# Decode attention plus MLP on one core: the last rows of w2 loaded in three even transfers instead of seven partly uneven ones, and the MLP's first bias in five transfers instead of one

## The chip, the core and the metric

The kernel runs on one core of a Trainium2 chip. The metric is the device time of one execution in microseconds (us), as the median over several executions. "The profile" is one execution recorded by the hardware profiler; its times count from the start of that execution's span.

## What is computed

The kernel is one decode step for two sequences (B = 2, one new token each, width D = 576): the input, plus attention over a sliding window of a key/value cache, plus an MLP with squared ReLU. Both branches read the same layer-normed input. All tensors are bf16.

```python
W = min(4096, max(256, Sk // 4))            # 2048 of the 8192 cached positions
xn = _layernorm(x)
q = xn @ wq                                 # [2, 576] @ [576, 4096], 32 heads of 128
k, v = last W positions of the caches       # 16 heads, each for two heads of q
o = softmax(q k^T * 128 ** -0.5) @ v
attn = o @ wo                               # [2, 4096] @ [4096, 576]
h = relu(xn @ w1 + b1) ** 2                 # [2, 576] @ [576, 4608]
mlp = h @ w2 + b2                           # [2, 4608] @ [4608, 576]
out = x + attn + mlp
```

There are only two rows of activations, so nearly all of the work is reading: 53.6 MB of caches and weights from HBM, each byte once.

## The kernel before

**Units.** The attention is cut into eight units (four groups of four key/value heads, times two sequences). Unit u has one 2 MB tile of K and one of V, `k_u` and `v_u`, each loaded by one transfer of 128 partitions x 16 KB. `step(u)` transposes K on TensorE in eight groups (`transposes`, copied out of PSUM by ScalarE in L276 and VectorE in L278), forms the scores and the softmax, and carries along the product with V of unit u - 2. K and V tiles share a pool of six buffers, so the load of a later tile waits until TensorE has read the tile whose buffer it takes.

**Weights.** `issue_flat` loads wq, w1 and wo (4.5 to 5.2 MB each) as one flat transfer each. w1 and wo use the buffer that wq had, so wo is issued when the first MLP product (`mlp_h`, which adds the bias b1 by a matmul) has read w1.

**w2.** Its 4608 rows are seen as two halves of 128 partitions x 18 rows (`w2_rows`); one row of one partition is 576 elements, 1152 B, and a partition's 18 rows of a half lie next to each other in HBM. The first half is one tile, `w2a` (20736 B per partition). The second half is split: rows 0 to 8 go to `w2b` (10368 B per partition, in a buffer of the K/V pool), rows 9 to 17 to `w2c`, a buffer of its own. `W2P` (L76) lists the pieces of `w2c` as ranges of rows, and `issue_w2c` (L215) issues them. The piece of rows 12 to 15 is issued as four transfers over the partition ranges of `XS`: 0 to 24, 25 to 29, 30 to 125, 126 to 127. All other pieces cover 128 partitions.

**Queues.** The large transfers are issued by SyncE, in the order k0, wq, k1, v0, k2, v1, k3, v2, ..., w1, k7, v6, v7, wo, w2a, w2b, then the pieces of w2c, and run in the profile's queue q1. ScalarE issues four small ones (queue q10): x, the bias b1 (L423; 8 rows of 1152 B), the bias b2 (L424) and the output. Every transfer signals one of eight DMA semaphores, which the tile framework hands out in turn over both queues, in the order in which it places the transfers. A transfer whose semaphore is still in use by the transfer eight places before waits on its issuing engine until that one has landed.

**The end.** `out_acc` multiplies a row of activations, one per partition, with one row of weights per partition and adds into `out_ps`: four matmuls of 144 columns. The order is: the 32 rows of wo, the 18 rows of w2a, then rows 0 to 17 of the second half, of which 0 to 8 read `w2b` and 9 to 17 read `w2c`. ScalarE copies `out_ps` (L459) and issues the output's transfer (L460).

```python
for r in range(FR):
    w, o = (w2b_sb, r) if r < R9 else (w2c_sb, r - R9)
    out_acc(hT_sb[:, 1, r, :], w, o, stop=(r == FR - 1))
```

Of the kernel before, what the change touches and what calls it, by code (L numbers as in the profile page):

```python
# [16 lines left out]
def kernel(  # L17
# [14 lines left out]
    nc = tc.nc  # L32
    P = 128
    B, Sq, D = A_x.shape
# [38 lines left out]
    WC = Dh // WR  # L73
    FR = L1 // P
    assert HW == 32 * FR and QH * 2 == NC and NC * WC == 32
    W2P = [(9, 12), (12, 16), (16, 17), (17, 18)]  # L76
    R9 = 9
    XR = (12, 16)
    XS = [(0, 25), (25, 30), (30, 126), (126, 128)]
    BS = 16  # L80
    MB = BS * (B - 1) + 1
    RM = 32 * (NG4 - 1) + MB
# [99 lines left out]
    for t0, half, k0, n, pc in ((0, 0, 0, NK, 0), (0, 1, 0, NK, 1), (1, 0, 1, NK - 1, 1), (1, 1, 0, NK - 1, 0)):  # L182
# [11 lines left out]
                          in_=own[:].unsqueeze(2).to_broadcast([P, NC, WC]))  # L194
# [11 lines left out]
                          in_=ident[0:2 * NG4, 0:2 * NG4].rearrange("p (x g) -> p x g", g=NG4).unsqueeze(3)  # L206
                          .to_broadcast([2 * NG4, 2, NG4, B]))

    b1_sb = const.tile([2 * NG4, HW], BF16, name="b1_sb")
    w2_rows = B_w2.rearrange("(x p r) n -> x p (r n)", x=2, r=FR)  # L210


    w2c_sb = w2pool.tile([P, (FR - R9) * D], BF16, name="w2c")

    def issue_w2c(r0, r1, q):  # L215
        for p0, p1 in XS if (r0, r1) == XR else [(0, P)]:
            q.dma_start(out=w2c_sb[p0:p1, (r0 - R9) * D:(r1 - R9) * D], in_=w2_rows[1, p0:p1, r0 * D:r1 * D])

    out_ps = psum.tile([RM, OQ], F32, tag="out", name="out_ps")
    nc.vector.memset(out_ps[:], 0.0)  # L220
# [172 lines left out]
    def step(u):  # L393
        fin = None
        w = u - 2
        with_pv = w >= 0
        for g in range(NG):
            transposes(u, g)
            if with_pv and g == 1:
                pv(w, 0, 2)  # L400
            if with_pv and g == 2:
                pv(w, 1, 2)
                fin = pv_end(w)
            if g == TG + 1:
                scores(u, 0)
            if g == TG + 2 and fin:
                fin()
        scores(u, 1)
        softmax(u)
# [10 lines left out]
    softmax(0)  # L420
    load_v(2)
    b1_rows = B_b1.rearrange("(x n) -> x n", n=HW)
    nc.scalar.dma_start(out=b1_sb[:], in_=b1_rows)  # L423
    nc.scalar.dma_start(out=xb_sb[B:B + 1, :], in_=B_b2.rearrange("(o n) -> o n", o=1))  # L424
    step(1)
    load_k(4)
# [16 lines left out]
    nc.sync.dma_start(out=w2a_sb[:], in_=w2_rows[0])  # L443
    nc.sync.dma_start(out=w2b_sb[:], in_=w2_rows[1, :, 0:R9 * D])
    for r0, r1 in W2P:
        issue_w2c(r0, r1, nc.sync)
    step(NU - 1)
    pv_all(NU - 2)
    pv_all(NU - 1)
# [41 lines left out]
```

## Time and profile before

| | |
|---|---|
| three executions | 135.7, 136.2, 136.22 us; median 136.2 |
| the profiled execution | 135.7 us, of which the span is 133.8 |
| read from HBM | 53.62 MB, 401 GB/s over the span |
| TensorE busy | 86.7 us, 65% of the span |
| VectorE, ScalarE busy | 63.0 and 46.5 us, 47% and 35% |
| DMA queue q1 (SyncE's transfers) | 95.1% of 16 engines' span |
| DMA queue q8 (instructions) | 7 packets, 0.3% |

The span's slices in the page are 1/40 of it each, 3.35 us. The row "DMA" gives the mean busy share of the core's 16 DMA engines in tenths, the row "GB/s" what they moved in that slice. The chain of work that ended last is followed back from the last instruction; its shares tell what the end was waiting for. A table of stages gives for each stretch the busy time of PE, PEld, DVE, ACT and POOL with the count of instructions, then the granted TensorE clock, the DMA share (1 is all 16 engines) and GB/s. In a list of instructions in order of time, the columns are start, duration, engine, line, operation and operands, and in brackets the idle time before it with what ended it. In a list of waits, the numbers after the colon are the total in us, how often, and the longest. Beside these views, the trace has a record of each DMA packet (start, duration, bytes, queue) and of each landing on a DMA semaphore.

### The profile page before, as it was taken

How to read it: one execution, taken by the hardware profiler on the slowest of the kernel's cores; microseconds unless marked ns; L12 is line 12 of the kernel's file. 1: busy time of each engine (PE TensorE's matmuls, PEld its weight loads, DVE VectorE, ACT ScalarE, POOL GpSimd, SP SyncE). 2: the span in 40 equal slices, each digit the busy share in tenths (PEclk: the TensorE clock that was granted, in tenths of full speed). 3: DMA queues.
4: the chain of work that ended last, by engine and by line, in shares of the span. 5: the costliest groups of instructions: out<-in, count | busy, mean ns of one | idle time of the engine just before them, and what ended most of it. 6: DMA issues, size and time to landing. Idle time of an engine off the chain costs nothing.

```text
span 133.8 us, 2285 instructions
## 1 busy us (share of the span) xinstructions
PE 86.7 (65%) x949; PEld 52.4 (39%) x949; DVE 63.0 (47%) x176; ACT 46.5 (35%) x67; POOL 4.9 (4%) x15
## 2 busy tenths in 40 slices
PE   0079429699589777796797986007659962469351
PEld 0069302266346353443363452004255621159230
DVE  7754400326457667496547496300364776620000
ACT  6715400328656185283535373200206522000000
POOL 5000000010010100100100100100000001000000
PEclk9999955558999999999779999755686998555955
DMA  4999899999999999999999999989999989899960
GB/s 148 397 439 518 364 406 431 431 431 421 433 431 426 441 416 436 426 436 426 436 421 431 466 505 409 402 385 416 446 416 476 457 375 507 382 409 396 307 168 1
DMA packets 3655, 53.76 MB, mean 402 GB/s; under 512 B 435, under 2 KB 702, under 8 KB 958
## 3 DMA queue, kind: packets, MB, share of 16 engines
q1 hardware_dynamic: 3612, 53.61, 95.1%
q8 instruction: 7, 0.11, 0.3%
q10 hardware_dynamic: 34, 0.02, 0.0%
q14 instruction: 2, 0.02, 0.0%
HBM read 53.62 MB, written 0.00 MB: 401 GB/s over the span
## 4 chain that ended last, share of the span: by engine, by line
DMA 74%; PE 15%; ACT 5%; DVE 2%; issue 1%; SPq 0%; POOL 0%; ACTq 0%; DVEq 0%
DMA v<-in_A_v_cache_dram 24%; DMA w2c<-in_B_w_dram 22%; DMA k<-in_A_k_cache_dram 15%; DMA wq<-in_A_wq_dram 13%; PE kT_ps L99 6%; PE q_ps L96 3%; ACT kT L276 3%; PE sc_ps L96 3%; PE o_ps L96 1%; ACT p L308 1%; ACT L308 1%; PE qT_ps L99 1%; PE out_ps L96 1%; DVE m L297 1%; DVE qrow L244 1%
## 5 line engine op out<-in xcount | busy, mean ns | idle before, releaser
L99 PE MATMUL kT_ps<-ident_f,k 128*128 128x128 f32 x256 | 41.2, 311 | 5.3 <-DMA k<-in_A_k_cache_dram 2.7
L99 PEld LDWEIGHTS kT_ps<-ident_f,k 128*128 128x128 f32 x256 | 32.6, 159 | 19.2 <-issue 8.8
L276 ACT COPY kT<-kT_ps 128x1024 bf16<-128x1024 bf16 x32 | 31.8, 1012 | 18.9 <-PE kT_ps L99 18.9
L278 DVE COPY kT<-kT_ps 128x1024 bf16<-128x1024 bf16 x32 | 21.8, 680 | 6.5 <-PE kT_ps L99 6.2
L96 PE MATMUL sc_ps<-kT,qz 128*32 128x512 bf16 x128 | 10.5, 413 | 6.5 <-DVE kT L278 4.7
L308 ACT ACTIVATE p<-sc_ps,bias 128x512 bf16<-128x512 f32 x8 | 5.5, 687 | 21.3 <-DVE gown L304 21.3
L96 PE MATMUL o_ps<-v,pT 128*32 128x512 bf16 x128 | 11.9, 454 | 0.0
L96 PEld LDWEIGHTS <-xnT 128*4 128x4 bf16 x108 | 3.6, 121 | 16.4 <-issue 14.8
L96 PE MATMUL h_ps<-w,xnT 128*4 128x288 bf16 x72 | 4.5, 443 | 8.0 <-DMA w<-in_B_w_dram 8.0
L311 DVE STREAM_TRANSPOSE pT<-p 128x512 bf16<-128x512 bf16 x8 | 5.7, 711 | 6.2 <-ACT p L308 6.2
L341 DVE SCALAR_TENSOR_TENSOR o<-o_ps,in_s,o 128x128 f32<-128x128 f32 x24 | 8.3, 345 | 0.4
L297 DVE TENSOR_REDUCE m<-sc_ps 128x1 f32<-128x512 f32 x8 | 5.5, 691 | 5.5 <-PE sc_ps L96 5.5
L381 DVE TENSOR_TENSOR hrow<-t 100x1152 bf16<-100x1152 f32 x2 | 2.6, 1354 | 9.7 <-ACT t L379 9.7
L459 ACT CAST fin_sb<-out_ps 113x144 bf16<-113x144 f32 x1 | 0.3, 278 | 19.1 <-PE out_ps L96 19.1
L96 PE MATMUL q_ps<-wq,xnT 128*4 128x512 bf16 x36 | 4.0, 627 | 4.4 <-DMA wq<-in_A_wq_dram 4.4
L301 POOL PARTITION_ALL_REDUCE gmax<-m x8 | 2.9, 365 | 105.4 <-DVE m L299 105.4
L96 PE MATMUL op_ps<-o,of_h 128*32 128x129 f32 x16 | 3.7, 316 | 4.6 <-DVE o L341 4.6
L96 PEld LDWEIGHTS <-qz 128*32 128x32 bf16 x128 | 2.2, 98 | 10.7 <-DVE kT L278 7.2
L99 PE MATMUL pro_ps<-ident,xn_sb 2*128 2x2 bf16 x5 | 0.9, 180 | 6.8 <-DVE xn_sb L173 6.5
L96 PEld LDWEIGHTS <-hT_sb 128*17 128x17 bf16 x144 | 3.3, 109 | 4.8 <-issue 4.8
L96 PE MATMUL out_ps<-wo,ws 128*17 128x144 bf16 x128 | 4.0, 324 | 1.2 <-DVE ws L357 1.2
L339 DVE TENSOR_SCALAR o<-o_ps,in_s 128x128 f32<-128x128 f32 x8 | 2.7, 341 | 3.7 <-PE o_ps L96 3.7
(71 smaller groups left out, 56.0 us busy)
## 6 DMA issues: line engine op xcount, KB each, us to landing
k<-in_A_k_cache_dram SPq DMA_DIRECT2D x8, 2048.0 KB, 21.2
v<-in_A_v_cache_dram SPq DMA_DIRECT2D x8, 2048.0 KB, 23.7
w<-in_B_w_dram SPq DMA_DIRECT2D x1, 5184.0 KB
wq<-in_A_wq_dram SPq DMA_DIRECT2D x1, 4608.0 KB
wo<-in_A_wo_dram SPq DMA_DIRECT2D x1, 4608.0 KB, 20.9
w2a<-in_B_w_dram SPq DMA_DIRECT2D x1, 2592.0 KB, 26.7
w2b<-in_B_w_dram SPq DMA_DIRECT2D x1, 1296.0 KB
w2c<-in_B_w_dram SPq DMA_DIRECT2D x2, 432.0 KB
```

What stands on the lines that cost most here:

```text
L96: tc.keep_in_program_order(nc.tensor.matmul(*a, **k))
L99: tc.keep_in_program_order(nc.tensor.transpose(*a, **k))
L244: cp(out=qrow[:, k * QW:(k + 1) * QW].rearrange("p (i a d) -> p i a d", a=2, d=Dh), in_=q_ps[0:RB, k * QW // 2:(k + 1) * QW // 2].rearrang ...
L276: nc.scalar.copy(out=kT, in_=kT_ps[:])
L278: nc.vector.tensor_copy(out=kT, in_=kT_ps[:])
L297: nc.vector.tensor_reduce(out=m1[:], in_=sc_ps[:], axis=AX.X, op=ALU.max)
L301: nc.gpsimd.partition_all_reduce(gmax[:], m2[:], channels=P, reduce_op=ReduceOp.max)
L308: nc.scalar.activation(out=p_sb[:], in_=sc_ps[:], func=ACT.Exp, bias=bias[:, 0:1], scale=scale, accum_out=o1[:, Dh:Dh + 1])
L311: nc.vector.transpose(out=pT[:].rearrange("p j r -> p (j r)"), in_=p_sb[:])
L339: nc.vector.tensor_scalar(scalar1=in_s[:, 0:1], scalar2=None, op0=ALU.mult, **kw)
L341: nc.vector.scalar_tensor_tensor(scalar=in_s[:, k:k + 1], in1=o1[:, 0:Dh], op0=ALU.mult, op1=ALU.add, **kw)
L381: nc.vector.tensor_tensor(out=h4[:, :, k * HB:(k + 1) * HB], in0=t4, in1=t4, op=ALU.mult)
```

## The change

Rows 9 to 17 of w2's second half are loaded in three transfers of 128 partitions each: rows 9 to 14 (6912 B per partition), 15 and 16 (2304 B), and 17 (1152 B). Before, they were loaded as rows 9 to 11, rows 12 to 15 in four transfers over unequal ranges of partitions, row 16 and row 17, seven transfers in all. The bias b1 is loaded in five transfers of 2, 2, 2, 1 and 1 rows instead of one of 8 rows. What is computed, and TensorE's instructions and their order, stay the same.

```diff
-    W2P = [(9, 12), (12, 16), (16, 17), (17, 18)]
+    W2P = [(9, 15), (15, 17), (17, 18)]
     R9 = 9
-    XR = (12, 16)
-    XS = [(0, 25), (25, 30), (30, 126), (126, 128)]
...
-
-    def issue_w2c(r0, r1, q):
-        for p0, p1 in XS if (r0, r1) == XR else [(0, P)]:
-            q.dma_start(out=w2c_sb[p0:p1, (r0 - R9) * D:(r1 - R9) * D], in_=w2_rows[1, p0:p1, r0 * D:r1 * D])
...
     b1_rows = B_b1.rearrange("(x n) -> x n", n=HW)
-    nc.scalar.dma_start(out=b1_sb[:], in_=b1_rows)
+    for i0, i1 in ((0, 2), (2, 4), (4, 6), (6, 7), (7, 8)):
+        nc.scalar.dma_start(out=b1_sb[i0:i1, :], in_=b1_rows[i0:i1, :])
...
     for r0, r1 in W2P:
-        issue_w2c(r0, r1, nc.sync)
+        nc.sync.dma_start(out=w2c_sb[:, (r0 - R9) * D:(r1 - R9) * D], in_=w2_rows[1, :, r0 * D:r1 * D])
```

## Prediction

> **What bounds the kernel now.** I read the page's slices first, then its chain, then the last 25 us as a table of stages, the waits, and last the trace's records of single DMA packets and of semaphore landings.
>
> ```profile
> DMA  4999899999999999999999999989999989899960
> GB/s 148 397 439 518 364 406 431 431 431 421 433 431 426 441 416 436 426 436 426 436 421 431 466 505 409 402 385 416 446 416 476 457 375 507 382 409 396 307 168 1
> q1 hardware_dynamic: 3612, 53.61, 95.1%
> DMA 74%; PE 15%; ACT 5%; DVE 2%; issue 1%; SPq 0%; POOL 0%; ACTq 0%; DVEq 0%
> ```
>
> From the second slice to the 37th the 16 DMA engines are full and move some 430 GB/s; q1 (SyncE's queue) carries nearly all of it. The kernel ends when the last bytes of w2 are in, plus a fixed tail. In slices 38 and 39 the engines still count as busy, yet the rate falls to 307 and 168 GB/s. The stages show that fall:
>
> ```profile
> 116.00:122.00 6.00, 3.78 (x110) 3.38 (x114) 1.74 (x6) 0.00 (x0) 0.00 (x0) 0.50 1.01 434
> 124.00:125.40 1.40, 0.06 (x2) 0.00 (x0) 0.00 (x0) 0.00 (x0) 0.00 (x0) 1.00 1.02 388
> 125.40:127.00 1.60, 0.81 (x31) 0.61 (x34) 0.00 (x0) 0.00 (x0) 0.00 (x0) 0.87 1.01 223
> 127.00:129.00 2.00, 1.30 (x44) 0.96 (x36) 0.00 (x0) 0.00 (x0) 0.00 (x0) 0.50 0.85 220
> 129.00:130.60 1.60, 0.74 (x29) 0.60 (x24) 0.00 (x0) 0.00 (x0) 0.00 (x0) 0.50 0.30 91
> ```
>
> The last two columns are DMA share and GB/s: from 125.4 us the engines are busy at half the rate. TensorE only follows:
>
> ```profile
> 126.67 1.26 PE L96 MATMUL out_ps<-w2b,hT_sb 128*17 128x144 bf16 x36 [0.50 <-DMA w2b<-in_B_w_dram]
> 128.64 0.54 PE L96 MATMUL out_ps<-w2c,hT_sb 128*17 128x144 bf16 x12 [0.70 <-DMA w2c<-in_B_w_dram]
> 130.03 0.90 PE L96 MATMUL out_ps<-w2c,hT_sb 128*17 128x144 bf16 x24 [0.86 <-DMA w2c<-in_B_w_dram]
> 130.98 0.28 ACT L459 CAST fin_sb<-out_ps 113x144 bf16<-113x144 f32 x1 [19.08 <-PE out_ps L96]
> ```
>
> Each group starts within 0.1 us of a landing. The last piece (row 17) lands at 130.51; TensorE ends at 130.93, 0.42 later, the span at 133.83.
>
> **Single packets.** One packet is one partition's share of a transfer. In full flow a packet of 10368 B (w2b) takes 389 ns, 3456 B (rows 9 to 11) 135, 4608 B (rows 12 to 15) 178, 1152 B 51: straight-line costs, about 26.9 GB/s per engine and a few ns. That holds for every stretch from 6 us up to 125.3. Then, on all engines at once, 3456 B take about 250, 4608 B 300 to 360, 1152 B 70 to 95, and the last 10368 B up to 635; only after 129.5 is 1152 back at 51. The slow stretch begins 0.6 us after the first packets of rows 12 to 15, the uneven loads.
>
> **Late engines.** A transfer's semaphore gets one landing from each engine that carries it. w2a's 16 landings run from 120.96 to 122.86: ten within 0.56 us, one at 0.95, five 1.68 to 1.90 late. The five come one by one, each after a 16 KB packet of the instruction queue (q8 in the page, seven packets, 0.92 to 0.96 us each, 1.29 for the last): k2's landings spread by 0.47 without the latest and by 1.79 with it, and the packet before it is an instruction fetch at 30 us. A sixth fetch at 123 makes a sixth late engine. The landing counts (5, 5, 16, 2) show how rows 12 to 15 are dealt out: 25 partitions over five engines, 5 over five, 96 over sixteen, 2 over two. So two engines move 13 partitions of these rows, three move 12 and eleven move 6, where an even load has 8.
>
> **What the change costs, part by part.**
>
> *Rows 9 to 17 in three even pieces.* I follow the latest engine of w2a, landed at 122.86. w2b: 8 packets x 389 + 9 ns for the semaphore = 3.12 us (the first engine needed 124.08 - 120.96 = 3.12). Rows 9 to 14 are packets of 6912 B, which the trace lacks: half way between 3456 (135) and 10368 (389) it is 262; 8 x 262 + 9 = 2.10. Rows 15 and 16, 2304 B, half way between 51 and 135: 93; 8 x 93 + 9 = 0.75. Row 17: 8 x 51 + 9 = 0.42. Sum 6.39, so the last landing is at 129.25 instead of 130.51: **-1.26 us**. This already includes the price of the lost balancing, which is 2 partitions x 171 ns of bytes = 0.34 us if the late engines are among the eleven. It rests on one choice: that even pieces run at the full-flow rates. The other bound takes the rates of 125.4 to 129, when 220 GB/s are moved whatever the pieces: then the bytes left at 125.4 need as long as now, the late engines carry two partitions of 4608 B more at about 320 ns (0.64 us), and some 0.2 us more is lost as the early ones run dry: **+0.8 us**. I take the first, because 3456 B packets ran at 135 for 1.5 us beside the late engines' 10368 B at 389, and the K/V flow with the same five late engines never slowed: engines out of step and short even packets are not enough.
>
> [...]
>
> *TensorE's end.* Both versions finish with row 17, 4 matmuls, so the 0.42 us stay. Rows 9 to 14 land at 122.86 + 5.22 = 128.08, 24 matmuls at 0.90 per 24 end by 129.0; rows 15 and 16 land at 128.83, 8 matmuls are done by 129.25. w2b lands at 125.98; TensorE's own stall in w2a (idle 1.64 us, no releaser, resumed at 125.69 after an instruction fetch) ends at 126.1, so w2b's 36 matmuls end at 127.4, before 128.08. Nothing new is late; if that stall were 1 us longer, the order would still hold.
>
> *Four transfers fewer on SyncE.* Its waits in L217 vanish; they held nothing up, as q1 was full behind them:
>
> ```profile
> SPq L217 <- DMA wo<-in_A_wo_dram: 10.7, 1, 10.7
> SPq L217 <- DMA w2a<-in_B_w_dram: 5.8, 1, 5.8
> 97.13 26.09 SPq L217 DMA_DIRECT2D w2c<-in_B_w_dram  x7
> ```
>
> Zero, with q1's backlog as the cover.
>
> *Bias in five transfers.* Four more issues on ScalarE's queue, each about 0.29 us:
>
> ```profile
> 4.44 0.29 ACTq L423 DMA_DIRECT2D b_sb<-in_B_b_dram  x1
> 9.51 1.01 ACT L276 COPY kT<-kT_ps 128x1024 bf16<-128x1024 bf16 x1 [3.59 <-PE kT_ps L99]
> ```
>
> 4 x 0.29 = 1.2 us, from 4.73 to 5.9; b2's issue moves to 6.3, ScalarE's next copy waits until 9.51 for TensorE. Its bytes go to two engines instead of eight: four more 1152 B packets and semaphores on the first, 4 x (51 + 9) = 0.24 us of that one's time, one of seven where it might turn late, so 0 to 0.24; I take 0. The pieces also turn the eight DMA semaphores: in the built program k1 now waits for k0, v0, k2 and v1 for bias pieces, k3 for wq. These gate issues on SyncE, and all its later issues stand behind them. k0 landed at 8.31; wq's packets last until 18.8. On the bias's engines its packets alternate with wq's of 1.36 us (data at 8.5, semaphore at 9.9, b2's data at 11.3), so the third piece lands near 16.1 (10.6 + 2 x 2.7) and v1 is issued then; k3 and v2 follow at 19.3. k1, v0, k2 and v1 hold the queue until 38. Zero, with 7 us to spare at v0's issue and more behind it.
>
> [...]
>
> **Sum.** The profiled execution took 135.7 (span 133.83 and 1.9 around it): 135.7 - 1.26 = 134.4. It is the fastest of the three runs; against the median of 136.2 the same step gives 135.0, and that is my number.
>
> **Rivals.** (a) Short packets at the end are slow by themselves, whichever partitions they go to: the +0.8 bound, 137.0. For it: 1152 B packets of plain even pieces were slow as well; against it: the 135 and 178 ns rows before 125.3. It decides if 6912 B packets take over 262 + 1260 / 8 = 420 ns on the late engines. (b) The seventh instruction fetch, now at 127.5 for 1.29 us, hits a late engine: a fetch cost an engine about 1.3 us (k2's 1.79 - 0.47), so the end is at 130.6 and the time 136.2. Against it: the first six fetches made six different engines late. (c) The turned semaphores starve q1 early on: v0 would have to be issued after 23.6, k1's landing; v0's wait, the first bias piece, came at 10.6. Each us of a gap is one of time; from 1.26 us on it eats the gain.
>
> **How the numbers follow.** Forecast 0.60: 135.0, its own range 134.3 to 135.5 (0.24 for the first engine, some 0.4 from run to run). (b) with other partial gains 0.20: 135.6 to 136.6. (a) 0.18: 136.5 to 137.5. (c) 0.02. Half a per cent, about what a measurement tells from no change, is 0.68 us. Faster by more: 0.60; within: 0.21; slower: 0.19. The range 134.3 to 137.0 leaves out the far end of (a) and luck on the fast side.
>
> **What would show it.** Right: 6912 B packets near 262 ns, 2304 B near 93, over 380 GB/s up to 127, the last DMA landing near 129.3, TensorE's last four matmuls 0.4 behind it, DMA share unbroken from 7 to 60 us. Wrong: rates of 220 GB/s after 125.4 without uneven pieces (a), one engine 1.3 us behind the other late ones (b), a hole in the DMA row before 40 us (c).

## The result, and the profile after

The changed kernel takes **134.05 us** (median of four executions, 133.98 to 134.06), the kernel before 136.21 (135.7 to 136.24): a ratio of **0.985, 95% interval 0.983 to 0.987**, so 1.5% faster. The forecast was 135.0 with a range of 134.3 to 137.0: the direction was right, the gain of 2.16 us is almost twice the forecast one (1.2), and the time lies 0.25 us below the range. The profiled executions are 134.06 us (span 132.2) and 135.7 (span 133.8), which differ by 1.64.

The slices of the page, of the changed kernel. DMA stays full to the 38th slice, as before, but slices 37 to 39 now move 442, 397 and 250 GB/s, where the kernel before moved 396, 307 and 168.

```profile
DMA  3999899999999999999999999998999999899960
GB/s 115 436 442 514 380 397 417 436 436 407 444 411 451 421 436 426 431 431 411 456 416 434 426 488 402 407 479 382 441 431 431 480 384 491 382 402 442 397 250 1
```

The stages of the end, changed kernel; the last two columns are DMA share and GB/s.

```profile
124.00:125.40 1.40, 0.45 (x18) 0.29 (x18) 0.00 (x0) 0.00 (x0) 0.00 (x0) 1.00 1.02 432
125.40:127.00 1.60, 1.17 (x38) 1.02 (x36) 0.00 (x0) 0.00 (x0) 0.00 (x0) 0.67 0.98 393
127.00:129.00 2.00, 1.16 (x38) 0.94 (x33) 0.00 (x0) 0.00 (x0) 0.00 (x0) 0.50 0.33 126
```

From 125.4 to 127 us a DMA share of 0.98 now moves 393 GB/s, where 1.01 moved 223. From 127 on the share itself drops: the landings of the last row run from 127.21 to 128.95, so the early engines are done and only the late ones still load. That is the picture of engines out of step but undisturbed.

TensorE's end, instructions in order of time:

```profile
125.87 1.24 PE L94 MATMUL out_ps<-w2b,hT_sb 128*17 128x144 bf16 x36 [0.43 <-DMA w2b<-in_B_w_dram]
127.95 1.35 PE L94 MATMUL out_ps<-w2c,hT_sb 128*17 128x144 bf16 x36 [0.84 <-DMA w2c<-in_B_w_dram]
129.34 0.28 ACT L454 CAST fin_sb<-out_ps 113x144 bf16<-113x144 f32 x1 [17.75 <-PE out_ps L94]
```

The matmuls on w2c now run as one group from 127.95 to 129.29; before, they ended at 130.93. The trace's records of single packets show what the interpolation said: 262 ns for 6912 B, 93 for 2304 B, 51 for 1152 B, each with no scatter at all over the 128 packets. The last landing of w2 is at 128.95.

### The profile page after: what moved, and what is told of

Same layout as the page of the kernel before. It is cut to its first block, busy times and chain, and to the rows that moved or that the text cites. A ratio compares the mean times of both kernels' runs of the same rounds, so it can differ in the third digit from the quotient of the medians.

```text
span 132.2 us, 2284 instructions
## 1 busy us (share of the span) xinstructions
PE 85.9 (65%) x949; PEld 53.0 (40%) x949; DVE 63.2 (48%) x176; ACT 46.7 (35%) x67; POOL 4.9 (4%) x15
## 3 DMA queue, kind: packets, MB, share of 16 engines
q1 hardware_dynamic: 3456, 53.61, 95.1%
## 4 chain that ended last, share of the span: by engine, by line
DMA 77%; PE 17%; SPq 1%; DVE 1%; ACT 1%; issue 1%; ACTq 0%; DVEq 0%
DMA w<-in_B_w_dram 24%; DMA w2c<-in_B_w_dram 23%; DMA k<-in_A_k_cache_dram 16%; DMA wq<-in_A_wq_dram 13%; PE kT_ps L97 7%; PE h_ps L94 3%; PE q_ps L94 3%; PE sc_ps L94 1%; PE o_ps L94 1%; PE out_ps L94 1%; DVE qrow L238 1%; SPq L106 0%; ACT qrow L238 0%; DVE qz L254 0%; SPq L438 0%
## 5 line engine op out<-in xcount | busy, mean ns | idle before, releaser
L97 PE MATMUL kT_ps<-ident_f,k 128*128 128x128 f32 x256 | 42.0, 316 | 5.6 <-DMA k<-in_A_k_cache_dram 4.1
L97 PEld LDWEIGHTS kT_ps<-ident_f,k 128*128 128x128 f32 x256 | 33.3, 162 | 19.1 <-issue 10.2
L94 PE MATMUL sc_ps<-kT,qz 128*32 128x512 bf16 x128 | 9.7, 383 | 6.7 <-DVE kT L272 4.7
```

Of the source, the lines that this page charges most:

```text
L94: tc.keep_in_program_order(nc.tensor.matmul(*a, **k))
L97: tc.keep_in_program_order(nc.tensor.transpose(*a, **k))
```

## The experiments

Theory A is the prediction's: transfers whose partitions are dealt out to the engines unlike those of a full transfer ("crossed" below) slow every DMA packet at the end. Against it stood: short pieces are slow by themselves (B), the unequal amounts cost, not the places (U), and the bias transfers carry part of the gain (C). Later came D (SyncE's last waits cost time in the kernel's last 3 us) with its rival E (its waits at the start do), and F (the late engines make the scatter of the kernel before). Where a mean time of packets, a landing or the end of TensorE is given without a line, it comes from the trace's records.

**Even load, old row pieces, old bias** (`even_same_rows`).

```diff
-    XS = [(0, 25), (25, 30), (30, 126), (126, 128)]
+    XS = [(0, P)]
```

> The kernel before, with the piece of rows 12 to 15 as one transfer over 128 partitions; row pieces (9-11, 12-15, 16, 17) and the single bias transfer stay. Theory A (the transfers over 25, 5, 96 and 2 partitions make all DMA packets of the end slow): packets at 135, 178 and 51 ns throughout, last landing near 129.0, time 134.0 to 134.3. Theory B (many short pieces at the end are slow by themselves): 3456 B at about 250 ns and 220 GB/s after 125.4 as before, time 136 or more.

Measured: 134.56 us (134.53 to 135.15), ratio 0.9905 (0.9876 to 0.9935). All 128 packets of 4608 B took 178 to 181 ns, those of 3456 B 135 to 139, of 1152 B 51; the last landing was at 129.23. Its stage:

```profile
125.40:127.00 1.60, 1.27 (x52) 1.08 (x47) 0.00 (x0) 0.00 (x0) 0.00 (x0) 0.68 1.03 403
```

The same short pieces run at 403 GB/s once they are even: B falls. A said 134.0 to 134.3 and the time was 0.26 above that; most of the rest is found in the kernel's last 3 us, below.

**Equal amounts, other partitions** (`quarters`).

```diff
-    XS = [(0, 25), (25, 30), (30, 126), (126, 128)]
+    XS = [(0, 32), (32, 64), (64, 96), (96, 128)]
```

> The kernel before with rows 12 to 15 in four transfers of 32 partitions each (0-31, 32-63, 64-95, 96-127): every engine carries 8 partitions as in an even load, but two from each quarter, so not the eight that it has in a transfer over 128. Theory A in the form 'an engine that writes other partitions than its usual ones slows the others': packets of 4608 B at 300 ns or more, last landing 130.5 or later, time 136.0 to 137.5. Theory U (the unequal number of partitions per engine is what cost, not where they lie): 134.0 to 134.4, packets at 178 ns.

Measured: 137.01 us (136.34 to 137.78), ratio 1.0073 (1.0052 to 1.0094); packets of 4608 B at 337 ns on average; last landing at 132.47. Two of its stages:

```profile
125.40:127.00 1.60, 0.67 (x30) 0.47 (x28) 0.00 (x0) 0.00 (x0) 0.00 (x0) 0.87 0.96 186
127.00:129.00 2.00, 0.97 (x35) 0.77 (x25) 0.00 (x0) 0.00 (x0) 0.00 (x0) 0.50 1.02 173
```

All sixteen engines land for each of the four transfers, by an estimate with 32 / 16 = 2 partitions each, and the rate is lower than in the kernel before (186 and 173 GB/s against 223 and 220). U falls: equal amounts do not bring the full rate back. That it is which partitions an engine carries that costs, and not how many, is then the author's reading of this, as the trace has no record of an engine's partitions.

**The same in mid-flow** (`w2a_halves`), the disputed cost by itself, on the changed kernel:

```diff
-    nc.sync.dma_start(out=w2a_sb[:], in_=w2_rows[0])
+    for p0, p1 in ((0, 64), (64, 128)):
+        nc.sync.dma_start(out=w2a_sb[p0:p1, :], in_=w2_rows[0, p0:p1, :])
```

> The changed kernel with w2's first half (2592 KB, in the middle of the full flow) in two transfers of 64 partitions each instead of one of 128; bytes, engines and packet sizes (20736 B, 771 ns) as before, only the partitions that an engine writes differ. [...] Theory A in a weaker form (only transfers that run beside others with another deal of the partitions slow): some packets slow, 0.5 to 3 us more. If unusual partitions cost nothing: 771 ns and 134.1, and the slow end of the kernel before needs another cause.

Measured: 142.61 us in one execution, 8.4 above the changed kernel on the same chip (134.17). Packets of 20736 B took 1561 ns on average (1015 to 2241) instead of 771. First a stage of full flow in the changed kernel, then four of this run's:

```profile
116.00:122.00 6.00, 4.10 (x122) 3.71 (x126) 1.46 (x5) 0.00 (x0) 0.00 (x0) 0.50 1.01 435
```

```profile
115.00:118.00 3.00, 1.17 (x7) 0.18 (x2) 1.55 (x6) 0.00 (x0) 0.00 (x0) 0.50 0.91 185
121.00:124.00 3.00, 2.04 (x68) 1.73 (x60) 0.00 (x0) 0.00 (x0) 0.00 (x0) 0.50 1.04 221
127.00:130.00 3.00, 0.00 (x0) 0.00 (x0) 0.00 (x0) 0.00 (x0) 0.00 (x0) 0.50 0.92 197
130.00:133.00 3.00, 1.42 (x52) 1.45 (x56) 0.00 (x0) 0.00 (x0) 0.00 (x0) 0.50 0.91 366
```

Busy engines (a share of 0.91 to 1.04), about half the rate (185 to 221 GB/s against 435), and back up to 366 once the halves are through: the slowing comes in mid-flow too, and no packet of the halves escapes it, as the fastest took 1015 ns. The 0.5 to 3 us of the weaker form are far exceeded. Of the 8.4 us, 6.2 are what w2a's packets take once (8 per engine of 771 ns) and so the price of doubling them; the other 2.2 come on top. Transfers beside it pay too: wo, queued ahead, had its latest landing at 118.85 instead of 116.57, while the halves' packets had begun at 114.54 on the early engines, and w2b's packets, queued behind, took 543 ns on average instead of 393. This is how 0.6 MB of uneven pieces could slow w2b and the other rows. With one transfer more, and each half 1296 KB, the run also says that neither many nor small transfers are needed for the slowing.

**The bias alone** (`bias_only`), on the kernel before:

```diff
-    nc.scalar.dma_start(out=b1_sb[:], in_=b1_rows)
+    for i0, i1 in ((0, 2), (2, 4), (4, 6), (6, 7), (7, 8)):
+        nc.scalar.dma_start(out=b1_sb[i0:i1, :], in_=b1_rows[i0:i1, :])
```

> The kernel before with the bias in five transfers, w2 as before. Theory A: the bias part is worth nothing, 136.2 (same as before within 0.3). Theory C (the bias transfers, through the turned DMA semaphores or the engines that carry them, brought the part of the gain that the sum of the prediction did not have, some 0.4 to 0.9 us): 135.3 to 135.8.

Measured: 136.39 us (135.83 to 136.81), ratio 1.0027 (1.0006 to 1.0048): 0.40 slower, where A allowed 0.3 and C had it faster. The last landing of w2 was at 130.53, as before, but from TensorE's end to the span's end it took 3.16 us instead of 2.90.

**The w2 part alone** (`w2_only`, and again beside the changed kernel as `w2_only_again`): the diff just shown, reversed, on the changed kernel.

> The changed kernel with the bias in one transfer again. Theory A: 134.05, same as the changed kernel within 0.3. Theory C: 134.5 to 134.9.

> The changed kernel with the bias in one transfer, as in the earlier run, on the same chip as the changed kernel. Theory A: equal to the changed kernel to 0.15. Theory C: 0.3 to 0.5 slower than it.

> The changed kernel, unaltered, beside its variants on one chip. Theory A (the w2 part is all of the gain): the same as with the bias in one transfer, to 0.15. Theory C (the bias part adds to it): 0.3 to 0.5 faster than that one, as 134.05 and 134.46 from two chips would have it. Both: its executions lie within 0.3 of each other, where those of the kernel before spread over 1.06.

Measured: 134.46 us, ratio 0.9888 (0.9867 to 0.991); again 134.42, 0.9881 (0.9849 to 0.9913); the changed kernel beside it 134.17 (134.04 to 134.78), 0.9863 (0.9832 to 0.9895). The medians differ by 0.25, between the two theories' numbers (up to 0.15, and 0.3 to 0.5), and the intervals overlap; the first 134.46, too, had lain between A's 134.35 and C's 134.5. That the changed kernel's executions keep within 0.3 of each other held for five of the six; the sixth took 134.78 with a span of 132.3 like the others, so its excess lies outside the span. The traces show where: w2's last landing (129.09 and 129.11) and TensorE's end (129.43 and 129.39) agree, but the rest of the span takes 3.18 us with one bias transfer and 2.89 with five. So C is wrong about the start of the kernel, and the bias does matter, at the end.

**Bias by columns** (`bias_columns`), on the changed kernel:

```diff
-    for i0, i1 in ((0, 2), (2, 4), (4, 6), (6, 7), (7, 8)):
-        nc.scalar.dma_start(out=b1_sb[i0:i1, :], in_=b1_rows[i0:i1, :])
+    for i0, i1 in ((0, 128), (128, 256), (256, 384), (384, 480), (480, 576)):
+        nc.scalar.dma_start(out=b1_sb[:, i0:i1], in_=b1_rows[:, i0:i1])
```

> The changed kernel with the bias in five transfers over columns (128, 128, 128, 96, 96), each of all 8 rows: as many transfers, semaphores and waits of SyncE as in the changed kernel, but spread over eight engines. Theory A: equal to the changed kernel to 0.15. Theory C by the turned semaphores: equal to the changed kernel and 0.3 to 0.5 faster than the bias in one transfer. Theory C by the engines that carry the bias: equal to the bias in one transfer.

Measured: 134.13 us (134.04 to 134.31), ratio 0.9857 (0.9829 to 0.9886), with 2.90 us after TensorE's end. Equal to the changed kernel, so the form of C by the engines that carry the bias falls: the number of transfers counts.

Where those 0.25 us lie is seen in SyncE's waits. It ends the program with five waits, each for two semaphores. Columns: total us, times, longest. First the changed kernel, then `w2_only`, with one bias transfer:

```profile
SPq L481 <- DMA w2b<-in_B_w_dram: 27.6, 1, 27.6
SPq L481 <- DMA w2c<-in_B_w_dram: 3.0, 3, 2.0
SPq L481 <- DMA out_dram<-fin_sb: 2.4, 1, 2.4
```

```profile
SPq L480 <- DMA out_dram<-fin_sb: 33.1, 1, 33.1
```

With 32 transfers in all, the output's signals the last of the eight semaphores, and SyncE gets through four waits while the loads come in. With 28, it signals the one in the first wait: SyncE stands there for 33 us, and the other four waits come after the output has landed, 0.062 to 0.069 us apart in the trace (131.614, 131.683, 131.751, 131.815, 131.877). The kernel before also had 32 transfers; `bias_only`, with 36, has the same fault as 28.

**Six bias transfers** (`bias_six`), as a test of that (D), on the changed kernel:

```diff
-    for i0, i1 in ((0, 2), (2, 4), (4, 6), (6, 7), (7, 8)):
+    for i0, i1 in ((0, 2), (2, 4), (4, 5), (5, 6), (6, 7), (7, 8)):
```

> The changed kernel with the bias in six transfers (2, 2, 1, 1, 1, 1 rows): 33 transfers instead of 32, so that the output's transfer signals the first of the eight DMA semaphores instead of the last. Theory D (SyncE waits for the eight semaphores one after the other at the end; those behind the output's cost about 0.063 us each, worked out from 0.25 us for four behind it with the bias in one transfer and 0.18 for three in the kernel with even pieces of the old rows): the last landing of w2 unchanged near 129.0, the time from TensorE's end to the span's end 2.90 + 7 x 0.063 = 3.34 us, time 134.5 to 134.6. Rival E (the waits at the start, k1 behind k0 and so on, make the difference between one and five bias transfers): 2.90 us after TensorE's end and 134.1.

Measured: 134.17 us (134.08 to 134.29), ratio 0.9869 (0.983 to 0.9907); 3.01 us after TensorE's end. Three of SyncE's last waits:

```profile
SPq L481 <- DMA w2a<-in_B_w_dram: 24.3, 1, 24.3
SPq L481 <- DMA out_dram<-fin_sb: 5.5, 1, 5.5
SPq L481 <- DMA w2b<-in_B_w_dram: 3.0, 1, 3.0
```

D's number of 0.44 us missed, because its order of the waits was wrong: they go in pairs, and the output's semaphore is now in the third of five, so two waits are left, not seven. Two are worth 2 x 0.063 = 0.13, the trace shows 3.01 - 2.90 = 0.11. E expected 2.90 and 134.1, and the median alone would fit it as well. Over the kernels, the time after TensorE's end is 2.89 to 2.91 with no wait left, 3.01 with two (`w2a_halves`, with 33 transfers, shows the same), 3.09 with three (even pieces, old rows: 29 transfers), 3.15 to 3.18 with four. A step of 0.1 us is seen in the traces, not in the medians.

**Three executions of the kernel before** (`before_look_a`, `_b`, `_c`), unaltered, for its scatter.

> The kernel before, unaltered, to see in a profile why its executions spread over 1.3 us of span (133.5 to 134.8) where even loads keep within 0.3. Theory A: the difference is all behind 124 us, in the packets of the end: last landing of w2 at the span minus 3.3 us, anywhere from 130.2 to 131.5, w2a's landing at 122.9 in all of them. Rival F (executions differ in the late engines, by where instruction fetches fall): w2a's last landing moves along with the span.

> A second execution of the kernel before; expectations as for the first.

> A third execution of the kernel before; expectations as for the first.

Measured: 135.97, 136.11 and 135.95 us. One stage of the first and one of the second, and the second's last matmuls:

```profile
125.40:127.00 1.60, 0.45 (x30) 0.27 (x22) 0.00 (x0) 0.00 (x0) 0.00 (x0) 1.00 0.98 218
```

```profile
127.00:129.00 2.00, 0.74 (x47) 0.59 (x35) 0.00 (x0) 0.00 (x0) 0.00 (x0) 0.66 0.87 211
```

```profile
130.43 0.90 PE L96 MATMUL out_ps<-w2c,hT_sb 128*17 128x144 bf16 x24 [1.11 <-DMA w2c<-in_B_w_dram]
```

w2a's last landing is at 122.91, 122.91 and 122.93, against 122.86 in the first profile. w2's last is at 130.69, 130.82 and 130.68, against 130.51; TensorE ends at 131.19, 131.33 and 131.18, against 130.93. So of the 0.24 to 0.40 us by which TensorE ends later, 0.05 to 0.07 stood there when w2a was in, 0.10 to 0.27 came from there to the last landing, and 0.07 to 0.08 behind that: mostly A, with a small share for F. The three spans, 134.1 to 134.2, cover only a part of the scatter from 133.5 to 134.8; its ends were not profiled. Their packets of 4608 B took 281, 286 and 278 ns on average, against 273.

## Why the prediction was right in direction and wrong in size

**The full-flow rates held, point by point.** 6912, 2304 and 1152 B packets took the 262, 93 and 51 ns of the sum. After 125.4 the rate was 393 GB/s, not 223. The two kernels with other crossed partitions show about half the rate (`quarters` 173 to 186 GB/s, `w2a_halves` 185 to 221), and the one that undoes only the unevenness (`even_same_rows`) shows 403. Rival (a), slow short pieces, is refuted by `even_same_rows`. Rival (b) did not come: the seventh instruction fetch, at 127.0 for 0.88 us, hit an engine that was not late, as the spread of the landings stays at 1.75 us from w2a to the last row (1.74). Rival (c) did not come either: v0 was issued at 10.71 us, v1 at 16.25, k3 at 19.20 and v2 at 19.85, as the working had it, and the DMA row has no hole.

**The step that failed is the last one, from the profiled execution to the median.** The working gave 134.4 for the changed kernel on the profiled execution (135.7 - 1.26), and then put the same step under the median of 136.2, for 135.0. But 135.7 was a good draw of a kernel whose end is a matter of luck: of its 41 executions beside the experiments, from 135.4 to 136.6 (spans from 133.5 to 134.8), nine were faster. What the three later profiles show of this scatter lies mostly behind w2a's landing, in the stretch that the change removes; `quarters`, also crossed at the end, scatters too (spans from 134.4 to 135.9). The even kernels hardly scatter in the span: 132.1 to 132.3 for the changed one, 132.2 to 132.3 by columns, 132.4 to 132.7 with one bias transfer. The sum was a sum for an undisturbed end, so it fixed the changed kernel's own time, whatever the kernel before happened to draw: 134.4 was the number to give. That is 0.5 of the 0.95 us by which the forecast missed (0.06 more is rounding, 134.94 to 135.0), and the range inherited it: "some 0.4 from run to run" was laid around the wrong centre. What the working set aside as "luck on the fast side" came in all four executions, 133.98 to 134.06; for the most part it was no luck.

**The other 0.38 us are in three terms of the sum.** The latest engine landed w2a at 122.73, not 122.86 (0.13; over the other profiles with w2a in one transfer it lies between 122.76 and 122.96, so this is a draw, and a lucky one). The steps between landings were 3.09, 2.08, 0.69 and 0.36, together 6.22 instead of 6.39 (0.17). On the latest engine a packet starts some 4 ns before the one ahead has ended (in row 17 packets of 51 ns start 47 ns apart), so durations, added up, come out about 0.03 too long for each of the four pieces; the rest is the time from a piece's last packet to its landing, 0.38 us in w2a and 0.33 in row 17. And TensorE ended 0.34 after the last landing, not 0.42 (0.08); in the profiles with crossed pieces at the end this is 0.34 to 0.54, in those with even ones 0.28 to 0.34. The working's line for a packet, 26.9 GB/s and a few ns, is also slightly off: 51 ns for 1152 B and 771 for 20736 B give 27.2 GB/s and 9 ns. No term of the sum hangs on that.

**Two zeros were zeros by cancelling.** "Four transfers fewer on SyncE" and "bias in five transfers" were each costed at nothing. The first alone costs 0.25 us (28 transfers, `w2_only`), the second alone about as much in the trace (36 transfers, `bias_only`), and both together nothing, as 32 - 4 + 4 is again 32. The prediction looked for the turned semaphores at the start, where the queue's backlog does cover them, and not at the program's last waits, where nothing does. What it got right was the cover at the start.

**What no run shows.** In `quarters` a 4608 B packet took 337 ns on average (178 to 548), and transfers over 64 partitions moved 185 to 221 GB/s, about half of the 435 of full ones. Why is not shown. That an engine carries other partitions in a crossed transfer than in a full one is the author's estimate from the counts of landings (25 partitions over five engines, 96 over sixteen), and no run separates the partitions that are written from the places in HBM that the engines read at the same time, which another deal would change too. Still open is why the first 20 uneven packets of the kernel before ran undisturbed (178 ns each) and all engines slowed at one moment, 125.3 us.

No variant here beats the changed kernel: `bias_columns` equals it, `bias_six` differs by 0.11 us in the trace alone, the others are slower.

## What to carry to other kernels

Before load is shifted between DMA engines by transfers over odd ranges of partitions, look at the duration of single packets: a DMA share of 1.01 at 223 GB/s, where full flow had 434, came here, from 125.4 to 127 us, with packets of 4608 B that took 294 to 360 ns instead of 178, and even transfers with some engines late were 1.6 us better in the two profiles. When a change removes a disturbed stretch, predict the changed kernel's own end from undisturbed rows; don't subtract the gain seen in one profile from a median over executions that the disturbance scatters. And count the transfers where the semaphores are handed out in turn: at the program's end, every wait behind the output's costs about 0.06 us.

## What the runs showed of the hardware that was not expected

- Two transfers over 64 of 128 partitions each, with all 16 engines busy, doubled the packet time (1561 against 771 ns on average) and slowed neighbouring full transfers too (w2b's packets 543 against 393 ns): 8.4 us more for 2592 KB that take 6.2 us when loaded evenly.
- Packets of the even pieces of the changed kernel repeat to the ns (262, 93, 51 in all of 128), with the engines 1.75 us out of step; in the other even runs they keep within 4 ns.
- After each of the first six instruction fetches of 16 KB one more engine was late, after the first fetch by about 1.3 us at once (k2's latest landing behind the next one); the late engines never caught up, and in the changed kernel (ten of w2b's landings from 124.08 to 124.95, six from 125.61 to 125.82) the latest of them sets the end, 1.74 us after the first. No run takes the fetches away, so that they are the cause is read from the order in time.
